# A first load in five parts of every 8th or 4th partition, two small loads moved to GpSimd, and a running sum that enters the last accumulators earlier

## The chip, the cores and the metric

One core of a Trainium2 chip runs the whole program. The metric is the device time of one execution in microseconds (us), lower being better. A ratio is the mean time of one kernel's fast runs over that of the other's fast runs of the same rounds, so it is not quite the ratio of the medians that are quoted. I turn a ratio into us by multiplying its excess by 134.2 us.

One correction holds for all that follows. The prediction took the times of single DMA packets from the trace's records with a zero that lies 0.23 us off: against the clock of the timeline, its packet times are 0.23 us too late (the first packet of K starts at 2.23 us, not 2.46; the last weight packet ends at 128.70 us, not 128.94). The document uses the timeline's clock; the recorded texts keep theirs.

## The reference, cut to what matters

A decode step for two sequences, one token each: layer norm, then the sum of the input, attention over the last 2048 cached positions, and a squared-ReLU MLP.

```python
xn = _layernorm(x, axis=-1)                  # x: (2, 1, 576)
return x + _A_ref(xn, A_k_cache, A_v_cache, A_wq, A_wo) + _B_ref(xn, B_w1, B_b1, B_w2, B_b2)
# _A_ref: 32 query heads, 16 K/V heads of 128, window W = 2048 of 8192 positions, all bf16
# _B_ref: h = xn @ w1 + b1;  out = relu(h)**2 @ w2 + b2;   w1 (576, 4608), w2 (4608, 576)
```

Hardly any of the 53.6 MB that are read is used more than once or twice, so it is a kernel of loads.

## The kernel before

The K and V windows are cut into eight units each of 2 MB, four heads of one sequence at a time. Partition `p = 4 * c + h` of a unit holds 64 consecutive positions (16 KB) of head `h`. SyncE issues the big loads in the order in which they are used.

```python
def unit_view(cache, u):
    tq, b = divmod(u, B)
    return cache[b, tq * TH:(tq + 1) * TH, S0:Sk, :].rearrange("h (c j) d -> c h (j d)", c=CP)   # TH = 4, CP = 32

def issue_kv(tiles, cache, u, name, parts=1):
    tl = kvpool.tile([P, UE], BF16, tag="kv", name=f"{name}_{u}")
    v = unit_view(cache, u)
    n = UE // parts
    tiles[u] = tl
    return [lambda i=i: nc.sync.dma_start(out=tl[:, i * n:(i + 1) * n], in_=v[:, :, i * n:(i + 1) * n])
            for i in range(parts)]
...
nc.scalar.dma_start(out=x_sb[0:B, :], in_=x2d)               # x
for g in range(2): nc.scalar.dma_start(...)                  # b1, two loads (cut)
for i in range(2): nc.scalar.dma_start(...)                  # b2, two loads (cut)
...
for f in issue_kv(k_tiles, A_k_cache, 0, "k"):               # the first K unit: one load of 128 partitions
    f()
issue_w(A_wq, "wq", QL)
...
load_k(1)
load_v(0)
```

At the end the running sum `out_ps` is copied to `part`, and small f32 matmuls bring it into the last four accumulators, between w2's rows 0 to 5 and 6 to 8 of the last group.

```python
for i in range(2):
    nc.vector.tensor_copy(out=part[:, i * OH:(i + 1) * OH], in_=out_ps[32 * i:32 * i + B, :])
mlp_tail(*W2P[NG4 - 1][1:])          # rows 0 to 5: 24 matmuls
for i in range(4):
    pe_mm(mlp["out"][32 * i:32 * i + B, :], lhsT=ident_f[0:B, 0:B], rhs=part[:, i * OQ:(i + 1) * OQ],
          start=False, stop=False, ...)
mlp_tail(*W2P[NG4][1:])              # rows 6 to 8: 12 matmuls
```

## Time and profile before

| | before |
|---|---|
| time, median of 3 | 134.11 us (134.08 to 134.57) |
| span of the profiled run | 132.3 us |
| first packet of the big loads | 2.23 us |
| end of the last weight packet | 128.70 us |
| TensorE, busy share | 67% |

### The profile page before, as it was taken

To read this page: it belongs to the slowest core of one execution; us is meant where nothing else is said; L and a number is where in the kernel's file an instruction comes from. 1 tells how busy PE (TensorE), PEld (TensorE's weight loads), DVE (VectorE), ACT (ScalarE), POOL (GpSimd) and SP (SyncE) were. 2 spreads that over 40 slices of the span, in tenths; PEclk is the share of its full clock that TensorE was granted. 3 is DMA by queue.
4 is the path that set the end of the run, shared out by engine and by line. 5 is a ranking of instruction groups with operands and counts; after the bars stand their busy time and mean duration, and the time that the engine had idled before them with its cause. 6 is when DMAs were issued, how large, how long until landed. Compare 5 with 4: busy or idle time off the path is not lost.

```text
span 132.3 us, 2040 instructions
## 1 busy us (share of the span) xinstructions
PE 89.0 (67%) x830; PEld 54.4 (41%) x830; DVE 59.6 (45%) x151; ACT 43.9 (33%) x63; POOL 7.7 (6%) x26
## 2 busy tenths in 40 slices
PE   0069319689862957699479989389703996499761
PEld 0059202629521355466174466064403661155430
DVE  6944400224640018555915685827730458644021
ACT  2716400015710136737236447145300651200001
POOL 7700000001000001010010010000010000000000
PEclk9999995955999599999968999977975699869999
DMA  4999989999998999999999999999999999999950
GB/s 139 394 461 468 423 381 431 436 466 514 414 401 352 436 416 451 416 446 426 426 431 426 436 421 443 416 435 431 432 436 426 431 433 439 411 420 429 421 230 1
DMA packets 3632, 53.74 MB, mean 406 GB/s; under 512 B 412, under 2 KB 420, under 8 KB 680
## 3 DMA queue, kind: packets, MB, share of 16 engines
q1 hardware_dynamic: 3604, 53.61, 95.0%
q8 instruction: 6, 0.10, 0.3%
q10 hardware_dynamic: 20, 0.01, 0.0%
q14 instruction: 2, 0.02, 0.0%
HBM read 53.62 MB, written 0.00 MB: 405 GB/s over the span
## 4 chain that ended last, share of the span: by engine, by line
DMA 70%; PE 22%; DVE 2%; ACT 2%; issue 1%; SPq 1%; DVEq 0%; ACTq 0%
DMA k<-in_A_k_cache_dram 42%; DMA w<-in_B_w_dram 14%; DMA wq_sb<-in_A_wq_dram 13%; PE kT_ps L86 11%; PE sc_ps L83 4%; PE q_ps L83 3%; PE pv_ps L83 2%; PE qs_ps L83 1%; DVE kT L286 1%; ACT kT L284 1%; ACT pr L323 1%; PE sm L83 1%; DVE qrow L250 1%; SPq L105 0%; DVE qz L266 0%
## 5 line engine op out<-in xcount | busy, mean ns | idle before, releaser
L86 PE MATMUL kT_ps<-ident_f,k 128*128 128x128 f32 x256 | 41.1, 317 | 12.4 <-DMA k<-in_A_k_cache_dram 11.8
L284 ACT COPY kT<-kT_ps 128x1024 bf16<-128x1024 bf16 x32 | 31.9, 1011 | 36.0 <-PE kT_ps L86 35.7
L86 PEld LDWEIGHTS kT_ps<-ident_f,k 128*128 128x128 f32 x256 | 34.0, 164 | 21.7 <-issue 18.2
L286 DVE COPY kT<-kT_ps 128x1024 bf16<-128x1024 bf16 x32 | 22.1, 691 | 31.5 <-PE kT_ps L86 31.4
L83 PE MATMUL sc_ps<-kT,qz 128*32 128x512 bf16 x128 | 10.5, 414 | 4.6 <-DVE kT L286 2.8
L83 PE MATMUL pv_ps<-v,pT 128*32 128x512 bf16 x128 | 11.9, 440 | 1.0 <-DVE acc L358 0.8
L312 POOL PARTITION_ALL_REDUCE gmax<-m x8 | 2.9, 366 | 103.1 <-DVE m L310 103.1
L323 ACT ACTIVATE pr<-sc_ps,nb 128x512 bf16<-128x512 f32 x8 | 5.5, 687 | 8.3 <-DVE nb L320 8.3
L83 PEld LDWEIGHTS <-xnT 128*4 128x4 bf16 x90 | 3.0, 110 | 12.0 <-issue 11.6
L83 PE MATMUL q_ps<-wq_sb,xnT 128*4 128x512 bf16 x36 | 3.8, 603 | 4.7 <-DMA wq_sb<-in_A_wq_dram 4.7
L308 DVE TENSOR_REDUCE mx<-sc_ps 128x1 f32<-128x512 f32 x8 | 5.5, 683 | 3.1 <-PE sc_ps L83 3.1
L83 PEld LDWEIGHTS <-qz 128*32 128x32 bf16 x128 | 2.3, 98 | 10.1 <-DVE kT L286 6.2
L83 PE MATMUL h_ps<-w_sb,xnT 128*4 128x384 bf16 x54 | 4.1, 443 | 3.2 <-DMA w_sb<-in_B_w_dram 3.2
L358 DVE SCALAR_TENSOR_TENSOR mix<-pv_ps,own_j,mix 128x128 f32<-128x128 f32 x16 | 5.6, 351 | 0.6
L564 ACT CAST fin_sb<-tail_ps 2x144 bf16<-2x144 f32 x2 | 0.5, 272 | 15.8 <-PE tail_ps L83 15.8
L329 DVE STREAM_TRANSPOSE pT<-pr 128x512 bf16<-128x512 bf16 x8 | 5.6, 703 | 0.2 <-ACT pr L323 0.2
L86 PE MATMUL pro_ps<-ident,xs 2*128 2x2 bf16 x10 | 0.6, 165 | 7.6 <-DVE xs L180 7.6
L83 PEld LDWEIGHTS <-pT 128*32 128x32 bf16 x128 | 2.9, 99 | 6.1 <-issue 3.7
L83 PE MATMUL out_ps<-wo_sb,ws 128*2 128x288 bf16 x64 | 5.0, 318 | 0.3 <-DVE ws L387 0.3
L83 PE MATMUL sm<-acc,tohead 128*64 128x129 f32 x16 | 3.7, 315 | 1.8 <-DVE acc L358 1.8
L83 PE MATMUL out_ps<-w,hT_sb 128*2 128x288 bf16 x54 | 3.8, 286 | 1.3 <-DMA w<-in_B_w_dram 1.3
L431 DVE TENSOR_TENSOR hs<-hT_ps,hodd 128x20 f32<-128x20 f32 (+1 forms) x4 | 0.5, 172 | 9.2 <-ACT hodd L428 9.2
(77 smaller groups left out, 58.2 us busy)
## 6 DMA issues: line engine op xcount, KB each, us to landing
k<-in_A_k_cache_dram SPq DMA_DIRECT2D x8, 2048.0 KB, 7.7
v<-in_A_v_cache_dram SPq DMA_DIRECT2D x8, 2048.0 KB, 18.1
w_sb<-in_B_w_dram SPq DMA_DIRECT2D x1, 5184.0 KB, 19.1
wq_sb<-in_A_wq_dram SPq DMA_DIRECT2D x1, 4608.0 KB
wo_sb<-in_A_wo_dram SPq DMA_DIRECT2D x2, 2304.0 KB
w<-in_B_w_dram SPq DMA_DIRECT2D x3, 1296.0 KB, 25.7
w<-in_B_w_dram SPq DMA_DIRECT2D x1, 864.0 KB
w<-in_B_w_dram SPq DMA_DIRECT2D x1, 432.0 KB
```

What stands on the lines that cost most here:

```text
L83: return tc.keep_in_program_order(nc.tensor.matmul(out, **kw))
L86: return tc.keep_in_program_order(nc.tensor.transpose(**kw))
L250: nc.vector.tensor_copy(out=qrow[:, 0, :], in_=q_ps[0][0:RB, :])
L284: pin(nc.scalar.copy(out=dst, in_=src))
L286: pin(nc.vector.tensor_copy(out=dst, in_=src))
L308: pin(nc.vector.tensor_reduce(out=mx[:], in_=sc_ps, axis=AX.X, op=ALU.max))
L312: nc.gpsimd.partition_all_reduce(gmax[:], m2[:], channels=P, reduce_op=ReduceOp.max)
L323: pin(nc.scalar.activation(out=pr[:], in_=sc_ps, func=ACT.Exp, bias=nb[:], scale=scale, accum_out=acc[:, Dh:Dh + 1]))
L329: pin(nc.vector.transpose(out=pT[:].rearrange("p t m -> p (t m)"), in_=pr[:]))
L358: op = nc.vector.scalar_tensor_tensor(out=nx, in0=pv_ps[:, j, :], scalar=own_j[:, j:j + 1], in1=acc, op0=ALU.mult, op1=ALU.add)
L431: nc.vector.tensor_tensor(out=hs[:].rearrange("p (g r) b -> p r g b", g=NG4)[:, r0:r0 + n, g:g + 2, :], in0=even[:, :, g:g + 2, :], in1=od ...
L564: cp(out=fin_sb[:, q * OQ:(q + 1) * OQ], in_=mlp["out"][32 * k:32 * k + B, :])
```

## The change

Intent: (1) let the first bytes flow sooner, by giving the first K unit as five loads, the first two of 16 partitions only; (2) take the small loads of b1 and b2 off ScalarE, and halve their number; (3) shorten the tail: the sum enters the accumulators before the last nine rows of w2, and the last load has two rows, not three.

```diff
-    def issue_kv(tiles, cache, u, name, parts=1):
+    def issue_kv(tiles, cache, u, name, first=False):
         tl = kvpool.tile([P, UE], BF16, tag="kv", name=f"{name}_{u}")
         v = unit_view(cache, u)
-        n = UE // parts
         tiles[u] = tl
-        return [lambda i=i: nc.sync.dma_start(out=tl[:, i * n:(i + 1) * n], in_=v[:, :, i * n:(i + 1) * n])
-                for i in range(parts)]
+        if not first:
+            nc.sync.dma_start(out=tl[:], in_=v)
+            return
+        for c in range(2):
+            nc.sync.dma_start(out=tl[TH * c:P:2 * TH, :], in_=v[c:CP:2, 0, :])
+        for h in range(1, TH):
+            nc.sync.dma_start(out=tl[h:P:TH, :], in_=v[:, h, :])
...
-    for g in range(2):
-        nc.scalar.dma_start(out=b1_sb[2 * g:2 * g + 2, :], ...)
-    for i in range(2):
-        nc.scalar.dma_start(out=x_sb[B:B + 1, i * OH:(i + 1) * OH], ...)
+    nc.gpsimd.dma_start(out=b1_sb[:], in_=B_b1.rearrange("(g n) -> g n", g=NG4))
+    nc.gpsimd.dma_start(out=x_sb[B:B + 1, :], in_=B_b2.rearrange("(o n) -> o n", o=1))
...
-    W2P = [(0, 0, 9), (1, 0, 9), (2, 0, 9), (3, 0, 6), (3, 6, 9)]
+    W2P = [(0, 0, 9), (1, 0, 9), (2, 0, 9), (3, 0, 7), (3, 7, 9)]
...
-    for i in range(2):
-        nc.vector.tensor_copy(out=part[:, i * OH:(i + 1) * OH], in_=out_ps[32 * i:32 * i + B, :])
-    mlp_tail(*W2P[NG4 - 1][1:])
+    for i, cp in enumerate((nc.vector.tensor_copy, nc.scalar.copy)):
+        cp(out=part[:, i * OH:(i + 1) * OH], in_=out_ps[32 * i:32 * i + B, :])
+    mlp["out"] = psum.tile([P, OQ], F32, tag="misc", name="tail_ps")
     for i in range(4):
         pe_mm(mlp["out"][32 * i:32 * i + B, :], lhsT=ident_f[0:B, 0:B], rhs=part[:, i * OQ:(i + 1) * OQ],
-              start=False, stop=False, skip_group_check=True, tile_position=(0, 32 * i))
+              start=True, stop=False, skip_group_check=True, tile_position=(0, 32 * i))
+    mlp_tail(*W2P[NG4 - 1][1:])
     mlp_tail(*W2P[NG4][1:])
```

More of the change, by code (lines that the diff above doesn't have):

```diff
@@ L134 @@
     b1_sb = const.tile([NG4, HW], BF16, name="b1_sb")
-    for g in range(2):
-        nc.scalar.dma_start(out=b1_sb[2 * g:2 * g + 2, :], in_=B_b1[2 * g * HW:2 * (g + 1) * HW].rearrange("(g n) -> g n", g=2))
-    for i in range(2):
-        nc.scalar.dma_start(out=x_sb[B:B + 1, i * OH:(i + 1) * OH],
-                            in_=B_b2[i * OH:(i + 1) * OH].rearrange("(o n) -> o n", o=1))
+    nc.gpsimd.dma_start(out=b1_sb[:], in_=B_b1.rearrange("(g n) -> g n", g=NG4))
+    nc.gpsimd.dma_start(out=x_sb[B:B + 1, :], in_=B_b2.rearrange("(o n) -> o n", o=1))
     eps_t = const.tile([B, 1], F32, name="eps_t")
@@ L143 @@
     nc.scalar.activation(out=warm[:, 0:1], in_=eps_t[:], func=ACT.Sqrt)
-    for f in issue_kv(k_tiles, A_k_cache, 0, "k"):
-        f()
+    issue_kv(k_tiles, A_k_cache, 0, "k", first=True)
     issue_w(A_wq, "wq", QL)
@@ L446, in mlp_tail @@
         w2_sb = w2_tiles.pop((NG4 - 1, r0))
-        if r0 == 0:
-            mlp["out"] = psum.tile([P, OQ], F32, tag="misc", name="tail_ps")
         for r in range(r0, r1):
@@ L452, in mlp_tail @@
                 pe_mm(mlp["out"][32 * i:32 * i + B, :], lhsT=mlp["h"][:, (NG4 - 1) * FR + r, :],
-                                 rhs=w2_sb[:, o + i * OQ:o + (i + 1) * OQ], start=(r == 0), stop=(r == FR - 1),
+                                 rhs=w2_sb[:, o + i * OQ:o + (i + 1) * OQ], start=False, stop=(r == FR - 1),
                                  skip_group_check=True, tile_position=(0, 32 * i))
     def load_k(u):
-        for f in issue_kv(k_tiles, A_k_cache, u, "k"):
-            f()
+        issue_kv(k_tiles, A_k_cache, u, "k")
     def load_v(u):
-        for f in issue_kv(v_tiles, A_v_cache, u, "v"):
-            f()
-    W2P = [(0, 0, 9), (1, 0, 9), (2, 0, 9), (3, 0, 6), (3, 6, 9)]
+        issue_kv(v_tiles, A_v_cache, u, "v")
+    W2P = [(0, 0, 9), (1, 0, 9), (2, 0, 9), (3, 0, 7), (3, 7, 9)]
     load_k(1)
```

## The prediction

The sum came to -0.39 us, so 133.7 us. The -0.49 us is an estimate: K's first packets trail x's by 0.59 us, and I took this to grow with the rows of a load, so that one of 16 rows would lose all but an allowance of 0.10 us. The +0.15 us is half of 0.3 us, by which the first packets were expected to take longer with 16 rows; no trace showed that beforehand. GpSimd's 0.00 us rested on an assumed time for its issues. Rival B stands as what it would cost, a doubling of the first unit's 4.9 us; its cause was not shown.

> **What bounds the kernel now.** I read, in this order, the page's engine shares, the row of DMA activity in forty slices, the queue list, the chain of work that ended last, the timeline of the first and the last microseconds, and the waits. The page first:
>
> ```profile
> PE 89.0 (67%) x830; PEld 54.4 (41%) x830; DVE 59.6 (45%) x151; ACT 43.9 (33%) x63; POOL 7.7 (6%) x26
> ...
> DMA  4999989999998999999999999999999999999950
> ...
> q1 hardware_dynamic: 3604, 53.61, 95.0%
> q8 instruction: 6, 0.10, 0.3%
> q10 hardware_dynamic: 20, 0.01, 0.0%
> ...
> DMA 70%; PE 22%; DVE 2%; ACT 2%; issue 1%; SPq 1%; DVEq 0%; ACTq 0%
> ```
>
> No compute engine passes 67%. The DMA row is near full in 37 of 40 slices; only the first (4) and the last two (5, 0) are not. The chain is 70% DMA. I then summed the trace's single packet records by microsecond: from 3 us to 127 us all sixteen DMA engines have a packet in work in every microsecond; the first packet of the big queue starts at 2.46 us and the last ends at 128.94 us. So nothing in the middle can help: 53.6 MB pass at about 430 GB/s, a 16 KB packet taking 0.611 us on its engine. The span of 132.3 us is 2.46 us before the first packet, 126.5 us of transfer, 3.4 us after it. The wait list shows the same: SyncE's waits in the middle are for PE to free buffers, but the issues stand far enough ahead that no engine runs dry. The change touches only the two ends, so they are read closely. The timeline at the start:
>
> ```profile
> 0.72 0.64 SPq L105 DMA_DIRECT2D k<-in_A_k_cache_dram  x1
> 0.72 0.55 ACTq L133 DMA_DIRECT2D x_sb<-in_A_x_dram  x1
> 0.75 1.15 POOL L166 MEMSET xs<- 2x1280 bf16 x1
> ...
> 1.30 0.64 ACTq L136 DMA_DIRECT2D b_sb<-in_B_b_dram  x2
> 1.42 0.57 SPq L110 DMA_DIRECT2D wq_sb<-in_A_wq_dram  x1
> ...
> 1.97 0.58 ACTq L138 DMA_DIRECT2D x_sb<-in_B_b_dram  x2
> ```
>
> and at the end:
>
> ```profile
> 127.37 0.93 DVE L553 COPY part<-out_ps 2x288 f32<-2x288 f32 x2 [5.90 <-PE out_ps L83]
> ...
> 128.13 0.55 PE L83 MATMUL tail_ps<-w,hT_sb 128*2 128x144 bf16 x24 [0.80 <-DMA w<-in_B_w_dram]
> ...
> 128.60 0.42 PE L83 MATMUL tail_ps<-part,ident_f 2*2 2x144 f32 x8
> ...
> 129.17 0.36 PE L83 MATMUL tail_ps<-w,hT_sb 128*2 128x144 bf16 x12
> ```
>
> At the start the K issue and the x issue leave their sequencers together, at 0.72 us. The first packets of x (two rows) start at 1.87 us, 1.15 us after the issue; those of K (128 rows of 16 KB on 16 engines) at 2.46 us, 1.74 us after it, spread over 0.25 us. At the end the last weights land at 128.94 us, PE goes at 129.17 us; the eight f32 matmuls on `part` were over at 129.02 us, so they already hide under that last transfer.
>
> [...]
>
> **The change, part by part.**
>
> *First K unit in five DMAs.* The first now has 16 rows,[...] not 128. [...]first packets at 0.72 + 1.15 + 0.10 = 1.97 us, a gain of 0.49 us. The supply must keep up: five issues of up to 0.64 us end at about 3.9 us, and wq's issue follows. Its first packet is there by about 3.9 + 1.74 = 5.7 us at the latest. K's eight packets per engine at 0.61 us, from 1.97 us on and with a slow first one of about 0.9 us, last until 1.97 + 0.9 + 7 x 0.61 = 7.1 us. So engines don't run dry; the later issues of the second K and first V hide under wq's 10.8 us. [...]
>
> *b1 and b2 by GpSimd, two DMAs for four.* ScalarE loses 0.64 + 0.58 = 1.2 us of issuing, so its table load starts about 1.2 us sooner; that is off the path, as normalisation waits for VectorE. GpSimd gains two issues[...], ahead of its clear of `xs`[...], while VectorE writes `xs` at 6.26 us. Nothing. [...]I followed the completion writes, and the last six engines end 128.5 to 128.9 us, the others from 127.5 to 128.0. Six is the number of 16 KB instruction packets (queue 8, about 0.9 us each) and they push back one engine each, as the staircase in the landings shows. I charge zero.
>
> *The tail.* `part` is made by two engines side by side: 0.45 us in place of 0.93, ready at about 127.8 us; its eight matmuls (0.42 us) end at about 128.3 us and free PE later. As they were hidden, this gains nothing by itself. The last load falls from three rows to two. Its last 295 KB take 0.69 us, so the seven rows ahead land at about 128.25 us and PE starts on them at about 128.5 us (0.25 us after, as for the last one today); 28 matmuls at 14 ns (24 take 0.55 us, the last alone 0.225) end at about 129.1 us. The last rows start at 129.17 us as today: just hidden. Eight matmuls instead of twelve save 4 x 12 ns = 0.05 us. The two casts, the store (issued at 130.21 us, written at about 131.3 us) and the close stay.
>
> Sum: -0.49 + 0.15 + 0.00 - 0.05 = -0.39 us; 134.11 - 0.39 = 133.72, say **133.7 us**, 0.3% down.
>
> **The rivals.**
>
> A. The delay of K's first packet is per engine[...], not per row. For it: K's first packets come one by one, some 16 ns apart[...]. Against it: that explains 0.25 of 0.59 us. Then the start gains nothing or 0.2 us, and the kernel ends at 133.9 to 134.1 us.
>
> B. [...]the unit's 4.9 us could double. Then the end goes up by at most 4.9 - 0.5 = 4.4 us, to 138.5 us. Against it: [...]such an odd pattern looks like one that was tried. Half in step would end at 135 to 136 us.
>
> C. GpSimd becomes the bound at the start: its two issues take far longer, the clear of `xs` comes after 6.26 us, and the transposes of K, behind it in PE's order, slip. They run 8.41 to 14.5 us and PE then idles until wq at 19.27 us, so 4.7 us of slip are free. No change in time.
>
> D. The seven-row load lands later than worked out, and PE reaches the last rows late: 0.1 us at most.
>
> **Range and chances.** The centre is the sum. Low end: the full 0.6 us at the start[...], a tail 0.1 us better, with a good run: 133.1. High end: A[...], with the scatter of 134.08 to 134.57 seen before: 134.4. Faster by 2% would need 131.4 us, which is more than the whole 2.46 us before the first packet could reasonably give: 2%. Slower by 2% (136.8 us) needs most of B: 6%. The rest, 92%, is within 2%.
>
> **What the profile afterwards should show.** First packets of the first K load near 2.0 us, and the first slice of the DMA row above 4; the five loads landed by about 7.8 us (8.25 now), with packets near 0.61 us; packets of 1.2 us there mean B, a first packet at 2.4 us means A. wq should land about 0.4 us before 19.2 us and every later wait on a DMA by as much; the last weights near 128.5 us; the last PE group with 8 matmuls starting about 0.2 us after that; no gap in the DMA row in between. If the end moved while the first packet did not, or the other way, my account is wrong.

## More of the kernel before

The rate of the DMA engines in forty slices of the span, GB/s, as the page has it for the kernel before:

```profile
GB/s 139 394 461 468 423 381 431 436 466 514 414 401 352 436 416 451 416 446 426 426 431 426 436 421 443 416 435 431 432 436 426 431 433 439 411 420 429 421 230 1
```

Each number stands for 3.3 us. The reader is to see that the rate is at its plateau from the second slice on; a number above or below its neighbours can come from the slice in which a large packet is counted. This program ends 3.64 us after its last weight packet (132.34 less 128.70).

## The result, and the profile after

The changed kernel took 135.95 us, median of 6 runs (135.54 to 136.41), against 134.10 us before (134.01 to 134.57): ratio 1.0131, 95% interval 1.0106 to 1.0156, that is +1.76 us (+1.4 to +2.1). The prediction had said -0.4 us, and its range ended at 134.4 us. Executions over 1.5% slower than the fastest of the same kernel are left out of the means.

The page of the changed kernel, its row of DMA activity, its rate and its queues:

```profile
DMA  4899999999998999999999999999999999999950
GB/s 120 279 416 439 417 392 449 410 522 413 420 445 370 420 435 425 435 430 435 425 430 425 439 420 444 417 432 438 428 425 435 435 422 432 422 417 436 416 204 1
...
q0 software_dynamic: 64, 0.01, 0.1%
q14 instruction: 2, 0.02, 0.0%
q10 hardware_dynamic: 8, 0.00, 0.0%
...
DMA 68%; PE 21%; ACT 3%; SPq 2%; DVE 2%; issue 1%; ACTq 0%; DVEq 0%
```

The activity row looks almost as before, with an 8 in the second slice. The rate does not: 120 and 279 GB/s in the first two slices, against 139 and 394. The engines are mostly busy, but bytes pass slowly. GpSimd's two loads appear as a queue of their own with 64 packets, where ScalarE's queue had 20 in all and now has 8.

The start of the timeline of the changed kernel:

```profile
0.72 0.54 ACTq L137 DMA_DIRECT2D x_sb<-in_A_x_dram  x1
0.72 1.25 SPq L108 DMA_DIRECT2D k<-in_A_k_cache_dram  x2
...
1.26 0.85 POOL L139 DMA_DIRECT2D b_sb<-in_B_b_dram  x1 [0.83 <-POOLq L577]
...
2.02 1.86 SPq L110 DMA_DIRECT2D k<-in_A_k_cache_dram  x3
2.12 0.53 POOL L140 DMA_DIRECT2D x_sb<-in_B_b_dram  x1
...
2.68 1.15 POOL L166 MEMSET xs<- 2x1280 bf16 x1
...
3.92 0.59 SPq L114 DMA_DIRECT2D wq_sb<-in_A_wq_dram  x1
```

The five K issues take SyncE from 0.72 to 3.88 us, as the prediction had it; wq is issued 2.5 us later than before (1.42 us). GpSimd's clear of `xs` ends at 3.83 us, in time for VectorE at 6.20 us, also as predicted.

To see the first unit itself, I read engine activity by stretches of two microseconds. The columns are the stretch, its length, five engines' busy time with their instruction counts, TensorE's granted clock, the busy share of the DMA engines, and GB/s. First the kernel before, then the changed one:

```profile
2.00:4.00 2.00, 0.00 (x0) 0.00 (x0) 1.82 (x9) 1.41 (x2) 0.94 (x2) 1.00 1.07 396
4.00:6.00 2.00, 0.00 (x0) 0.00 (x0) 2.00 (x9) 1.31 (x3) 1.84 (x8) 1.00 0.93 371
6.00:8.00 2.00, 0.37 (x7) 0.29 (x8) 1.75 (x4) 0.54 (x2) 0.54 (x3) 1.00 1.32 564
```

```profile
2.00:4.00 2.00, 0.00 (x0) 0.00 (x0) 1.82 (x9) 1.98 (x3) 1.99 (x5) 1.00 0.98 267
4.00:6.00 2.00, 0.00 (x0) 0.00 (x0) 1.80 (x10) 1.86 (x4) 2.00 (x8) 1.00 0.95 296
6.00:8.00 2.00, 0.42 (x10) 0.34 (x10) 1.69 (x3) 0.00 (x0) 1.12 (x5) 1.00 0.91 320
```

A packet is counted here where it starts, hence busy shares above 1. For six microseconds the changed kernel moves some 270 to 320 GB/s. From the single packet records, with a packet's bytes spread over its duration, I worked out where the time goes. The records do not name a packet's engine, so "per engine" is a sum over all packets divided by sixteen. "Rounds" are the unit's 128 packets of 16 KB in order of start, sixteen at a time:

```
                                    before          changed
first packet of K                   2.23 us         2.13 us
mean packet time by round, us       0.88 0.63 0.62 0.72   0.89 1.00 0.97 0.68
                                    0.61 0.64 0.61 0.61   0.74 0.82 0.64 0.63
packet time per engine, whole unit  5.31 us         6.37 us   (+1.06)
idle time per engine, up to 15 us   0.13 us         0.56 us   (+0.43)
MB landed by 15 / 60 / 120 us       5.27 24.61 50.36  4.58 23.93 49.67
```

The deficit is 0.69 MB at 15 us and 0.69 MB at 120 us, which is 1.6 us at 432 GB/s. So nearly all of the loss is made by 15 us and carried unchanged to 120 us. The last weight packet ends at 130.54 us, 1.84 us later than before; the span grows by 1.9 us. (The idle time depends on where one starts to count: other counts give 0.4 to 0.55 us more than before.)

The rounds tell more. Of the 1.06 us, 0.72 us lies in rounds 2 and 3, the second load of 16 rows and the round behind it, and 0.31 us in rounds 5 and 6, well inside the loads of 32 rows.

The tail of the changed kernel:

```profile
129.69 0.42 PE L83 MATMUL tail_ps<-part,ident_f 2*2 2x144 f32 x8 [0.53 <-DVE part L549]
...
130.32 1.01 PE L83 MATMUL tail_ps<-w,hT_sb 128*2 128x144 bf16 x36 [0.20 <-DMA w<-in_B_w_dram]
...
131.35 0.62 DVE L561 CAST fin_sb<-tail_ps 2x144 bf16<-2x144 f32 x2 [1.71 <-PE tail_ps L83]
```

The sum now comes first. The timeline merges all 36 matmuls into one group; the chain that ended last shows that the last eight still wait for the last load. Its last step on TensorE, first before, then after:

```profile
129.17 0.46 PE tail_ps L83 x12
```

```profile
131.03 0.40 PE tail_ps L83 x8
```

The casts start 0.81 us after the end of the last weight packet; before they started 0.85 us after (129.55 less 128.70). The tail neither caused nor cured anything of size.

### The profile page after: what moved, and what is told of

Same layout as the page of the kernel before. It is cut to its first block, busy times and chain, and to the rows that moved or that the text cites. A ratio compares the mean times of both kernels' runs of the same rounds, so it can differ in the third digit from the quotient of the medians.

```text
span 134.2 us, 2047 instructions
## 1 busy us (share of the span) xinstructions
PE 87.9 (66%) x830; PEld 54.9 (41%) x830; DVE 59.0 (44%) x150; ACT 46.8 (35%) x66; POOL 9.0 (7%) x28
## 4 chain that ended last, share of the span: by engine, by line
DMA 68%; PE 21%; ACT 3%; SPq 2%; DVE 2%; issue 1%; ACTq 0%; DVEq 0%
DMA k<-in_A_k_cache_dram 41%; DMA w<-in_B_w_dram 14%; DMA wq_sb<-in_A_wq_dram 13%; PE kT_ps L86 10%; PE sc_ps L83 4%; PE q_ps L83 3%; PE pv_ps L83 2%; PE qs_ps L83 1%; ACT kT L284 1%; SPq L110 1%; ACT L323 1%; SPq L108 1%; PE sm L83 1%; ACT pr L323 1%; DVE kT L286 1%
## 5 line engine op out<-in xcount | busy, mean ns | idle before, releaser
L86 PEld LDWEIGHTS kT_ps<-ident_f,k 128*128 128x128 f32 x256 | 34.7, 166 | 25.3 <-issue 21.8
L83 PEld LDWEIGHTS <-ws 128*2 128x2 bf16 x64 | 3.2, 98 | 2.8 <-DVE ws L387 0.6
L355 DVE TENSOR_SCALAR mix<-pv_ps,own_j 128x128 f32<-128x128 f32 x8 | 2.8, 345 | 3.4 <-PE pv_ps L83 3.4
```

The source lines that it names most:

```text
L83: return tc.keep_in_program_order(nc.tensor.matmul(out, **kw))
L86: return tc.keep_in_program_order(nc.tensor.transpose(**kw))
L355: op = nc.vector.tensor_scalar(out=nx, in0=pv_ps[:, j, :], scalar1=own_j[:, j:j + 1], scalar2=None, op0=ALU.mult)
```

## The experiments

The theories after the result were these. M: the five loads cost it all. P: a load of every 8th partition has stretched packets because of the partitions that it writes. S: the five small loads reach the engines late, and packets that come late are slow. P and S are suppositions; the causes that were put behind them no run shows. Rival G put it on GpSimd's 64 packets; E on the end of each extra load. Eighteen kernels were run.

### The three parts alone

Five loads alone (edit to the kernel before, inside `issue_kv`):

```diff
+        if name == "k" and u == 0:
+            for c in range(2):
+                nc.sync.dma_start(out=tl[TH * c:P:2 * TH, :], in_=v[c:CP:2, 0, :])
+            for h in range(1, TH):
+                nc.sync.dma_start(out=tl[h:P:TH, :], in_=v[:, h, :])
+            return []
```

> The kernel before with the five-DMA first K load alone. Changed kernel: 1.85 us slower than before, with 1.06 us more packet time and 0.43 us more idle time per DMA engine in the first 12 us. Theory M (the five loads cost it all[...]): +1.6 to +2.0 us, K packets of the first three rounds again near 0.9 to 1.0 us. Rival G (GpSimd's 64 small packets[...] slow the first packets): +0.3 to +0.9 us and packets back near 0.62 us after the first round.

Measured: 136.37 us, ratio 1.0156 (1.0120 to 1.0192), +2.1 us. The rounds took 0.89, 0.92, 1.13, 0.74, 0.92, 0.67, 0.66, 0.61 us. The five loads alone cost all of it and a little more.

GpSimd's two loads alone:

```diff
-    for g in range(2): nc.scalar.dma_start(out=b1_sb[2 * g:2 * g + 2, :], ...)
-    for i in range(2): nc.scalar.dma_start(out=x_sb[B:B + 1, i * OH:(i + 1) * OH], ...)
+    nc.gpsimd.dma_start(out=b1_sb[:], ...)
+    nc.gpsimd.dma_start(out=x_sb[B:B + 1, :], ...)
```

> The kernel before with b1 and b2 issued by GpSimd, nothing else. Theory M: within 0.2 us of before (134.1 us), K packets unchanged (5.3 us of packet time per engine for the unit). Rival G: +1 us or more, K packets stretched to 0.9 us where the small ones pass.

Measured: 134.56 us, ratio 1.0031 (1.0013 to 1.0048), +0.4 us. K's packets took 5.49 us per engine (5.31 before). This is more than theory M allowed and less than G's 1 us. It is a small cost of its own, not the cause; "Why the prediction was wrong" says where it arises.

The tail alone: the parts of the change that touch the tail, nothing else.

> The kernel before with the new tail alone (sum enters first, seven rows and two). The prediction said -0.05 us. Theory M: within 0.15 us of before, either way; the last group of PE starts when the last weights have landed plus 0.2 us. A rival, that the 36 matmuls now queue behind the landing of seven rows (the changed kernel shows one group of 36 taking 1.01 us): +0.2 to +0.4 us.

Measured: 134.06 us, ratio 0.9988 (0.9974 to 1.0002), -0.16 us (-0.35 to +0.03), not resolved from nothing. The casts of its profiled run start 0.67 us after the last weight packet (129.40 less 128.73), not 0.85.

The changed kernel with the first K unit back in one load:

```diff
-    issue_kv(k_tiles, A_k_cache, 0, "k", first=True)
+    issue_kv(k_tiles, A_k_cache, 0, "k")
```

> The changed kernel with the first K unit back in one load: GpSimd's b1 and b2 and the new tail stay. From the parts (+0.42 us for GpSimd's loads, -0.16 us for the tail): +0.1 to +0.4 us against before. If the five loads need GpSimd's part to be slow, or the other way (a cost shared between parts), the sum of parts fails: at or below before, or over +0.8 us.

Measured: 134.59 us, ratio 1.0024 (1.0003 to 1.0046), +0.3 us, as the sum of the two small parts. So taking back the five loads takes back nearly the whole loss.

### Partitions or supply

Five loads of the same sizes by columns, so that each reaches all partitions:

```diff
+            for a, z in ((0, 1), (1, 2), (2, 4), (4, 6), (6, 8)):
+                nc.sync.dma_start(out=tl[:, a * UE // 8:z * UE // 8], in_=v[:, :, a * UE // 8:z * UE // 8])
```

> The kernel before, first K unit in five DMAs of the same sizes (256, 256, 512, 512, 512 KB), but each of all 128 partitions and an eighth or a quarter of the columns[...]. Theory P[...]: idle time of about 0.4 us per engine stays, packet time per byte is normal (a 16 KB worth of packets 0.62 to 0.68 us after the first), end +0.3 to +0.7 us. Rival S (the pace of issues starves the engines, 256 KB per 0.65 us being just under the rate): +1.5 us or more, as in the changed kernel.

Measured: 136.91 us, ratio 1.0194 (1.0173 to 1.0216), +2.6 us: a miss for theory P, which had at most +0.7. It seemed to settle the case for supply. But its packets are small (2 and 4 KB), a handful of them took 0.5 to 1.8 us, and in the profiled run the last matmuls were slower (24 took 0.89 us, 0.55 us before), so that 0.68 us of the loss came after the last weights. So it needed counterparts in which one thing at a time is different.

The five partition loads on the second K unit (`u == 1`), which queues behind wq:

> The kernel before with the second K unit, not the first, in the same five loads of every 8th or 4th partition; it queues behind wq, some 10 us of transfer ahead of the engines. Theory S (late supply[...]): packets of this unit stay at 0.61 us, end within 0.2 us of before. Rival P[...]: its packets are stretched to 0.9 to 1.2 us and the end comes 1 us or more later. Rival E (each extra load costs its end on each engine): [...]+0.4 to +1.2 us.

Measured: 135.40 us, ratio 1.0088 (1.0063 to 1.0113), +1.2 us. SyncE issued the last of these loads at about 9.7 us, and the engines came to them at 18.35 us. With some nine microseconds in hand supply can't be late, yet the first three rounds took 0.77, 1.07 and 0.94 us, and the rest 0.61 to 0.63. Theory S alone is refuted as to these 1.2 us, of which 0.97 us is packet time of this unit (5.86 us per engine in place of 4.89).

The first unit as two loads of 64 partitions:

```diff
+            for c in range(2):
+                nc.sync.dma_start(out=tl[c * P // 2:(c + 1) * P // 2, :], in_=v[c * CP // 2:(c + 1) * CP // 2, :, :])
```

> The kernel before with the first K unit in two loads of 64 partitions,[...] 1 MB each, so supply (0.65 us for 2.4 us of transfer) is no matter. Theory S: within 0.3 us of before. Rival P: packets of the first half near 1.2 us, [...]+0.5 us at least.

Measured: 138.65 us, ratio 1.0328 (1.0300 to 1.0355), +4.4 us.

The same number and size of loads, but of half of the columns each:

```diff
+            for a, z in ((0, 4), (4, 8)):
+                nc.sync.dma_start(out=tl[:, a * UE // 8:z * UE // 8], in_=v[:, :, a * UE // 8:z * UE // 8])
```

> The kernel before, first K unit in two loads of 1 MB as with the two halves, but of all 128 partitions and half the columns[...]. Theory P[...]: 8 KB packets at about 0.31 us after the first, within 0.4 us of before, against +4.4 us with the two halves. Rival E (each extra load costs): no better than a large part of +4.4 us.

Measured: 134.13 us, ratio 0.9997 (0.9970 to 1.0024): nothing. The stretches from 4 to 8 us, first of the halves by partitions, then of those by columns (columns as above):

```profile
4.00:6.00 2.00, 0.00 (x0) 0.00 (x0) 2.00 (x9) 1.43 (x3) 1.83 (x8) 1.00 1.29 264
6.00:8.00 2.00, 0.37 (x8) 0.29 (x9) 1.75 (x4) 0.54 (x2) 0.54 (x4) 1.00 0.83 183
```

```profile
4.00:6.00 2.00, 0.00 (x0) 0.00 (x0) 2.00 (x10) 1.38 (x3) 1.84 (x8) 1.00 0.96 396
6.00:8.00 2.00, 0.37 (x8) 0.29 (x9) 1.75 (x4) 0.54 (x2) 0.54 (x3) 1.00 1.42 604
```

With half of the partitions five of the eight rounds took 1.25 to 1.28 us in place of 0.611, the others 0.98 to 1.14: with a packet's bytes spread over its duration, 212 to 219 GB/s from 2 to 12 us. So a load of 64 neighbouring partitions went at about half of the 432 GB/s; through what, no run shows. With all partitions the same two loads cost nothing, so neither a second load nor its end is what costs.

The five loads shared between two issuers (cut: b1, b2 and ScalarE's first activation moved behind wq):

```diff
+            for c in range(2):
+                (nc.sync, nc.scalar)[c].dma_start(out=tl[TH * c:P:2 * TH, :], in_=v[c:CP:2, 0, :])
+            for h in range(1, TH):
+                (nc.scalar if h == 2 else nc.sync).dma_start(out=tl[h:P:TH, :], in_=v[:, h, :])
```

> The five first loads, two of them (every 8th from 4, every 4th from 2) issued by ScalarE beside SyncE's three; b1 and b2 wait until after. Theory S: [...]the stretched packets and the idle time shrink and the end moves from +2.1 us (five loads alone) to between 0 and +1.0 us. Rivals P and E: no better than the five loads alone, +1.6 us or more.

Measured: 136.24 us, ratio 1.0137 (1.0103 to 1.0172), +1.8 us. This run can't be read as I meant it. In the trace of the kernel before, the 32 loads and stores of SyncE and ScalarE signal eight different semaphores, in turn, and the ninth, the first V load at 2.63 us, has a wait on the semaphore that x's load signals; the changed kernel's trace shows the same with its own eight. Here SyncE's wait list has 2.4 us on a K load before wq, which it issued at 5.20 us, so one lateness had been swapped for another. Inconclusive.

### The semaphores, and 16 or 32 rows

The same wait stands in the run of the five loads alone. The wait list of SyncE up to 8 us, of that run:

```profile
SPq L109 <- DMA k<-in_A_k_cache_dram: 0.9, 1, 0.9
```

x and the four small loads of b1 and b2 had taken five of the eight, so the fifth K load had to wait for the first one. In the changed kernel SyncE's wait list shows no such wait up to 15 us: in its trace GpSimd's two loads signal two semaphores outside these eight. Merging b1 and b2 into two loads that stay on ScalarE takes it away too:

```diff
-    (four loads of b1 and b2 on nc.scalar)
+    nc.scalar.dma_start(out=b1_sb[:], ...)
+    nc.scalar.dma_start(out=x_sb[B:B + 1, :], ...)
     (with the five first loads)
```

> Five first K loads, b1 and b2 in two loads in place of four but still by ScalarE. Ten loads no longer stand before wq, so the fifth K load finds a free semaphore of the eight. If that wait made the rest of the cost: SyncE's five issues without the gap of 0.9 us, idle engines as in the changed kernel, +1.2 to +1.7 us against before (five loads alone: +2.1 us). If the wait cost nothing: +2.0 us or more again.

Measured: 136.35 us, ratio 1.0139 (1.0113 to 1.0164), +1.9 us. The gap in SyncE's issues is gone (wq at 3.98 us, 4.77 us with the wait). The time lies between what the two theories expected, and its interval overlaps that of the five loads alone. So the wait is real, but no cost of it is shown.

The second unit by four loads of 32 rows:

```diff
+        if name == "k" and u == 1:
+            for h in range(TH):
+                nc.sync.dma_start(out=tl[h:P:TH, :], in_=v[:, h, :])
```

> Second K unit by four loads of every 4th partition (32 rows[...]). [...]If only loads of 16 rows[...] are slow: within 0.2 us. If loads of fewer than 128 rows are slow as such: +1.2 us or more.

Measured: 134.36 us, ratio 1.0001 (0.9975 to 1.0028). Every round took 0.611 us. Loads of 32 rows cost nothing there, and of the five loads on the second unit it is then the two of 16 rows that cost.

The second unit by eight loads of 16 rows, in two orders:

```diff
+            for p in (0, 1, 2, 3, 4, 5, 6, 7):      # the other run: (0, 4, 1, 5, 2, 6, 3, 7)
+                nc.sync.dma_start(out=tl[p:P:2 * TH, :], in_=v[p // TH:CP:2, p % TH, :])
```

Of each expectation the first outcome is theory P's.

> Second K unit by eight loads of every 8th partition, in the order 0, 1, 2, 3, 4, 5, 6, 7[...]. [...]packets of 1.2 us nearly throughout, +3.5 to +5 us, as with the two halves. If a load's shape or number is what costs[...]: the same as the next run, within 0.5 us.

> The same eight loads in the order 0, 4, 1, 5, 2, 6, 3, 7[...]. [...]+0.8 to +2 us, at least 2 us less than in the other order. If shape or number costs: as in the other order.

Measured: 139.16 us, ratio 1.0355 (1.0330 to 1.0380), +4.8 us, with packets at 1.22 to 1.26 us; and in turn 137.97 us, ratio 1.0268 (1.0240 to 1.0295), +3.6 us, with packets at 1.05 to 1.07 us. The order counts, by 1.2 us. But the second order missed the expectation, by which it should have been at least 2 us quicker: its packets stayed at 1.05 us, steady from round to round.

The stretches 18 to 20 and 20 to 22 us, while the second unit lands, of the kernel before, of the five loads there, of four loads of 32 rows, of eight of 16 rows in the first order and of those in turn:

```profile
18.00:20.00 2.00, 0.73 (x8) 0.24 (x11) 0.00 (x0) 0.00 (x0) 0.00 (x0) 0.83 0.90 385
20.00:22.00 2.00, 2.00 (x24) 0.73 (x20) 0.00 (x0) 0.00 (x0) 0.00 (x0) 0.50 0.97 418
```

```profile
18.00:20.00 2.00, 0.36 (x4) 0.10 (x7) 0.00 (x0) 0.00 (x0) 0.00 (x0) 0.50 0.93 262
20.00:22.00 2.00, 2.00 (x24) 0.69 (x20) 0.00 (x0) 0.00 (x0) 0.00 (x0) 0.50 0.97 336
```

```profile
18.00:20.00 2.00, 0.93 (x12) 0.36 (x15) 0.00 (x0) 0.00 (x0) 0.00 (x0) 0.70 0.93 393
20.00:22.00 2.00, 2.00 (x24) 0.58 (x20) 0.00 (x0) 0.00 (x0) 0.00 (x0) 0.50 0.92 393
```

```profile
20.00:22.00 2.00, 2.00 (x24) 0.59 (x20) 0.00 (x0) 0.00 (x0) 0.00 (x0) 0.50 1.04 213
```

```profile
20.00:22.00 2.00, 2.00 (x24) 0.70 (x20) 0.00 (x0) 0.00 (x0) 0.00 (x0) 0.50 1.04 254
```

The last number of a line is the rate: 418 GB/s before, 336 where the last of the two 16-row loads pass, 393 with 32 rows, 213 and 254 with 16 rows all the way.

Is it the step of 8 partitions or the 16 rows, then? The next kernel puts the rows in wrong partitions, in steps of 7.

```diff
+            for p in range(8):
+                dst = tl[p:p + 7 * 15 + 1:7, :] if p < 7 else tl[112:P, :]
+                nc.sync.dma_start(out=dst, in_=v[p // TH:CP:2, p % TH, :])
```

> Wrong results on purpose: the second K unit by seven loads of 16 rows in steps of 7 partitions[...] and an eighth load of partitions 112 to 127[...]; sources, sizes and number as in the two runs with steps of 8. [...]the first seven rounds of packets at 0.61 to 0.75 us for most engines, a few near 1.2 us, only the eighth slow. If 16-row loads are slow as such: 1.05 us and more throughout, as with steps of 8.

Measured in one look, of unknown state: 138.23 us. By the order of the start times, mean packet times were 0.68, 0.99, 1.02, 0.97, 0.80, 0.83 and 1.01 us, and 1.6 us in the next two groups, in which the eighth load and the first packets behind it pass. (It passed the comparison although K's rows were misplaced, so that comparison is not sensitive to this.) The stretch 20 to 22 us of this run, to hold against the last two above:

```profile
20.00:22.00 2.00, 2.00 (x24) 0.59 (x20) 0.00 (x0) 0.00 (x0) 0.00 (x0) 0.50 1.02 270
```

Theory P asked for most packets at 0.61 to 0.75 us. In the second round not one of the sixteen is below 0.95 us. So these loads of 16 rows are slow, mostly at 0.8 to 1.0 us a packet, in steps of 7 too; with the same sources in the same order but steps of 8 packets took 1.22 to 1.26 us, so the partitions seem to count as well (one look). What happens in the extra 0.2 to 0.4 us, no run here shows.

That it is the number of rows is not shown either. Two rivals stand untested: all loads of 16 rows read every second 16 KB of a head, which those of 32 rows do not, and how the rows are shared among the engines, which these traces do not show, may differ from load to load. And a run further down speaks against a rule about few rows: the load of 120 rows was slow too (1.23 us in the mean).

### Where the rest of it is

The five column loads on the second unit, to compare with the same loads at the start. The packet times of this expectation fit those of the trace before, where 2304 bytes took 93 ns and 3456 bytes 135 ns:

> The kernel before, second K unit in five column loads[...] (256, 256, 512, 512, 512 KB) behind wq. Partition loads at this place cost +1.2 us. Theory P: [...]this one costs only its smaller packets (5.16 for 4.89 us per engine, from 84 ns per 2 KB and 159 ns per 4 KB): +0.2 to +0.5 us. Rival E or a cost of many loads in flight: +1 us or more.

Measured: 134.90 us, ratio 1.0058 (1.0029 to 1.0087), +0.8 us, where the same five loads at the start cost +2.6 us. The partition loads showed +1.2 and +2.1 us. In both shapes, five loads at the very start cost 0.9 to 1.8 us more than the same five far ahead of their use; two loads of half the columns at the start cost nothing. (Of the 1.8 us, some 0.4 us came after the last weights, as the profiled runs of the two show, with slower last matmuls in the one at the start.) That much of theory S stands: five loads at the start have a price of their own. Through what, no run shows.

### Two looks at the first packet

x issued by SyncE after K, b1 and b2 after wq. The first outcome is for the case that K's first packet waits because of x's load:

```diff
-    nc.scalar.dma_start(out=x_sb[0:B, :], in_=x2d)   # and the four loads of b1 and b2, ahead of K
+    nc.sync.dma_start(out=x_sb[0:B, :], in_=x2d)     # between K and wq; b1 and b2 by nc.sync after wq
```

> The kernel before with x issued by SyncE between the first K load and wq, b1 and b2 behind wq, nothing by ScalarE at the start. The step of the prediction about 1.74 us from K's issue to its first packet is tested. [...]K no longer waits behind x: first packet 0.3 to 0.5 us sooner (1.9 to 2.1 us), end 0.2 to 0.5 us sooner. If the delay belongs to K's own 16 engines: first packet at 2.35 to 2.46 us, end within 0.2 us of before.

Measured: 134.22 us, ratio 1.0000 (0.9976 to 1.0024); K's first packet at 2.14 us. K had not been waiting behind x.

A first load of 8 rows, and one of the other 120 rows. I expected the 8 rows to pass through fewer engines; the records don't name them:

```diff
+            for a, z in ((0, 2), (2, CP)):
+                nc.sync.dma_start(out=tl[TH * a:TH * z, :], in_=v[a:z, :, :])
```

> The kernel before, first K unit in a load of 8 rows[...] and a second of the other 120 rows. Only the first packet counts; the time will be poor. If the time from issue to first packet grows with the engines told: 1.1 to 1.3 us (first packet at 1.85 to 2.0 us), as x with its two engines, not 1.65. If SyncE's path is simply slower than ScalarE's: 1.6 us or more (first packet at 2.3 us or later).

Measured in one look, of unknown state: first packet at 2.97 us, 2.25 us after the start of the issue, later than with any other split (142.85 us in all). The first expectation fails. The second holds by its words ("or later"), but a SyncE path that is simply slower doesn't explain why this load is later than the others from SyncE. From the end of the issue to the first packet it took 0.37 us for x's two rows, 0.87 us for 128 rows of K (before), 0.79 us for 16 (changed kernel) and 1.40 us for 8 (here). What sets this time stays open.

This run shows one thing more. The packets of the unit took 1.23 us in the mean (0.63 to 1.87), and nearly all of them belong to the load of 120 rows.

### The version that the experiments point to

One first load, the new tail, and x after K:

> The candidate: one first K load, the new tail, x issued by SyncE after K and the small loads after wq. From the parts (-0.16 us for the tail, 0.0 for x after K): -0.1 to -0.3 us against before, at the edge of what five rounds resolve, and 2 us better than the changed kernel.

Measured: 134.19 us, ratio 1.0000 (0.9982 to 1.0018). It beats the changed kernel by what that one lost, and is no better than the kernel before; the expected gain of 0.1 to 0.3 us is not resolved. The tail alone (0.9988) is the best of all, and its gain is not resolved either.

## Why the prediction was wrong

**The bound** was right: the kernel is set by the bytes, and a deficit at 15 us is the same deficit at 120 us (0.69 MB).

**The step that failed** is the first part of the change, "First K unit in five DMAs", in three of its terms.

- "a gain of 0.49 us": on the prediction's clock the first packet came at 2.36 us, not 1.97 (2.13 and 1.74 on the timeline's). Against the profile of before that is 0.10 us; but in five other kernels with one first load or with x moved (tail alone, GpSimd alone, x after K, one load back, the candidate) it also lies at 2.12 to 2.14 us, so the 16 rows gained nothing. The guess that the 0.59 us were a cost per row fell. Rival A was right that the term is nothing; its reason, a cost per engine, is not shown, and the load of 8 rows, half as many as there are engines, with the latest first packet of all (2.97 us), speaks against it.
- The charge of 0.15 us for slower first packets: the stretched packets cost 1.06 us per engine. The mis-sized term is the packet time, above all of the two loads of 16 rows. In these and the round behind them packets take about 1.0 us for 0.61, shown on the second unit (0.97 us more packet time per engine, and none more with four loads of 32 rows). I had charged for the first packets alone. The 0.31 us in rounds 5 and 6 of the first unit are in loads of 32 rows, which cost nothing on the second unit; that they come from the place at the start is argued only.
- "So engines don't run dry": they did, 0.43 us per engine more than before. I had compared the ends of the issues with the engines' need for the unit as a whole, not load by load.

**Rival B** named the size, "135 to 136 us", for half of its doubling; the result was 135.95 us. That hit is luck. Loads of 32 rows, which it feared, are free on the second unit (0.611 us a packet). Those of 16 rows are slow in steps of 8 (up to 1.26 us) and also in steps of 7 (mostly 0.8 to 1.0 us). That the number of rows is not all, the two halves (1.27 us a packet) and the two orders (1.2 us apart) show; B's cause they do not show.

**GpSimd**: the clear of `xs` was in time, as predicted (3.83 us for 6.20). "Nothing" was too little: +0.4 us alone and +0.3 us with the tail. The records of the sequencers show that most of it arises at the very end. With GpSimd's loads alone the output has landed at 131.47 us (131.51 before), but the program ends 1.15 us after that, not 0.84. At its end SyncE goes through a list of waits on the loads' semaphores, some 0.06 us for each entry (at 130.59, 130.66 and 130.72 us before). Before, the output's entries stand last in the list; with GpSimd's loads alone, or with the five loads alone, four more entries come behind them, 0.25 us. GpSimd's own closing takes 0.07 us longer. In the changed kernel the output's entries stand last again, and its end comes 0.91 us after the landing.

**The tail**: "0.05 us" of gain lies within -0.16 us, interval -0.35 to +0.03, which doesn't tell it from nothing; the last step of the chain is 0.06 us shorter, as worked out (0.40 for 0.46 us).

**A reading that was wrong** without harm to the sum: the packet times were 0.23 us late. So x's first packet came 0.92 us after the start of its issue, not 1.15, and K's 1.51, not 1.74. The 0.60 us that I had read from the end of x's issue to its first packet are 0.37 us. The 0.59 us between x and K stay.

At first sight the parts don't add: +2.1 for the five loads and +0.3 for the rest make 2.4 us, the changed kernel has 1.8. In the profiled runs the list at the end accounts for it: the five loads alone hold 0.25 us of it and the rest 0.3 us, the changed kernel only the 0.07 us of GpSimd. Without it, 1.8 and 0.0 us stand against 1.7 us. It does not touch the comparison of the five loads at the start with those on the second unit, which both have the four entries.

## What to carry to other kernels

When a kernel's DMA engines are busy from end to end, a busy row can still hide loss: look at the time of single packets, and at the bytes landed by a fixed moment. Cut a large load in a way whose packets you have seen at full pace: here all 128 rows, and 32 rows in steps of four on the second unit, took 0.611 us for 16 KB; 16 rows in steps of eight or seven (mostly 0.8 to 1.26 us), 64 neighbouring rows (0.98 to 1.28 us) and 120 rows (1.23 us in the mean, one look) did not. No rule by the number of rows alone fits all of these. A small first load meant as a quick start was paid for in slow packets here, and it did not even start sooner. Test a suspected load shape far ahead of its use as well as where it stands: the difference between the two is what its place costs.
